# Attention, ELU and SiLU layers: VectorE's side work by budget, silu by ScalarE, y pieces kept back, sums by way of DRAM

## The chip, the cores and the metric

One core of a Trainium2 chip. The metric is device time in microseconds (us), the median of the runs. Engines: TensorE (PE; its weight loads PEld), VectorE (DVE), ScalarE (ACT), GpSimd (POOL), and SyncE (SP), whose queue issues almost all DMAs.

## The reference

Windowed causal attention with a linear bias (4 batches, 8 heads, 576 positions, head size 64), then two feed-forward layers on the 2304 tokens of width 512, each through a hidden width of 2048:

```python
scores = scale * np.matmul(q, k.transpose(0, 1, 3, 2))
mask = (rel >= 0) & (rel < 128)
scores = np.where(mask, scores + bias[None], -1000000000.0)
attn = softmax(scores)                       # exp, sum + 1e-9, divide
x = np.matmul(attn, v)                       # -> 2304 x 512
h = x @ w_in;  g = np.where(h > 0, h, np.exp(np.minimum(h, 0)) - 1);  x = g @ w_out     # layer 0
h = x @ w_in2; g = h * (1 / (1 + np.exp(-h)));                        y = g @ w_out2    # layer 1
```

Weights arrive as 64-bit floats. The kernel makes 32-bit ones of them on the chip, and every product of a feed-forward layer is three matmuls on upper and lower parts (h times gh, h times gl, lo times gh).

## The kernel before

**Attention.** 18 tiles of 128 tokens, in 36 units (a pair of tiles, a pair of heads). The loop over u (39 turns) does scores of u, normalising of u - 1, transposes of u - 2 (`turn`) and, each second turn, the mixing with v (`mix`). Between them, `point` puts up to four pieces a turn from the list `fill` into TensorE's queue: pieces of layer 0's first sweep, for the token blocks that are ready (five blocks, one of 256 and four of 512 tokens). A block has 16 h pieces (4 hidden tiles by 4) and 16 y pieces; one is three matmuls of 512 columns. What follows a piece on other engines (`bent`, `gated`, `upper`, `lower`: Exp, ELU, upper part, lower part) is put out a step at a time by `pop`. What is left of `fill`, and the last block, are done at the start of `layers`.

**Layers.** The tokens are three blocks of 768. The hidden width is cut into sweeps: 4, 6 and 6 tiles in layer 0 (the first one in the attention), 6, 6 and 4 in layer 1. A step k (k0 to k14) is one block in one sweep. It has `quad`s, one for two hidden tiles: a 2 x 2 block product by seven products m1, m2, m6, m5, m7, m4, m3 (Strassen's way, with Winograd's sums), six matmuls of 384 columns each. Its operands are seven sums of x (`make`: sums and upper and lower parts of halves of x, by VectorE and ScalarE). A step whose block was made before in this layer reloads the seven from DRAM (`reload`); one that follows on the same block keeps them. Block order: 0, 1, 2, 2, 1, 0 in layer 0, then 2, 1, 0, 0, 1, 2, 2, 1, 0. After the quads come the y pieces (`outputs`), six matmuls each, and VectorE adds their sums into `acc`.

**Order around them.** The program's order on each engine is the order in which Python issues it. After every piece `between` is called: `chain` issues one step of every open activation (line 776: bent, gated, upper, lower), in y pieces three entries of `xtasks` (the sums of the next block) follow, and `weight_step` moves weights on a stage: load, rescale (GpSimd and ScalarE), sign, join (VectorE), part (upper by ScalarE, lower by VectorE; for a pair of kind 0 four sums as well). Raw weights have four buffers, pairs three (`PAIRS`), parted out-weights seven (`OUTS`). Nothing there looks at how much VectorE has already been given. What `xtasks` still holds is issued in one go after the y pieces, and weights that a step lacks are issued in one go ahead of it. `begin` loads a half of x into the one buffer `xs`; the second half (`begin(1)`) comes after all splits of the first.

Lines: 146 and 148 rescale, 153 sign, 158 join, 167 and 168 split of weights, 189 to 192 a pair's sums, 246 and 247 split of x in the attention, 263 multiplication or maximum of the activation, 277 and 313 h and y pieces of the first sweep, 452 scores, 491 transposes, 499 and 501 their copies, 530 mixing, 684 load of x, 692 to 706 sums, 761 first ScalarE step of an activation, 771 and 774 its upper and lower part, 794 products, 881 y.

## Time and profile before

| | us |
|---|---|
| median of 3 runs | 975.95 (974.37 to 976.24) |
| the profiled execution | 972.32 |
| its span | 970.3 |
| TensorE busy | 879.8 |
| VectorE busy | 655.6 |
| ScalarE busy | 506.6 |
| GpSimd busy | 136.9 |

The profile gives each engine's busy time, for any stretch of the span; the granted clock of TensorE (1 is 2.4 GHz, 0.5 is 1.2 GHz; a number between is a mean); and for every idle time of an engine the instruction that ended it. A busy TensorE may still run at the lower clock. Some matmul records are missing from the trace, so counts are a little low.

### The profile page before, as it was taken

The page shows a single profiled execution, that of the slowest core. Times are in us where ns is not written, and L with a number is a line of the kernel's source. Part 1 is how long each engine was busy: PE and PEld are TensorE (multiplying, and loading weights), DVE is VectorE, ACT ScalarE, POOL GpSimd, SP SyncE. Part 2 cuts the span into 40 slices and gives each one's busy share as a digit, 9 for nine tenths or more (in the row PEclk, how much of TensorE's full clock was granted, in tenths as well). Part 3 has the DMA queues.
Part 4 walks back from the last instruction along what each step waited for, and adds up shares of the span by engine and source line. Part 5 has one row for each costly group of instructions (what it writes and reads, how often), then busy time and mean ns, then how long its engine had stood idle before and what let it go on. Part 6 is the DMA issues. An engine that isn't in the chain of part 4 may idle for free.

```text
span 970.3 us, 15097 instructions
## 1 busy us (share of the span) xinstructions
PE 879.8 (91%) x5520; PEld 782.0 (81%) x5520; DVE 655.6 (68%) x1471; ACT 506.6 (52%) x1191; POOL 136.9 (14%) x248
## 2 busy tenths in 40 slices
PE   6788999996469998999999878999999999999998
PEld 4566777775459998988999778798989798889997
DVE  6866566638788767987545987856687652775544
ACT  6677667645564636554434636555656251634322
POOL 7753323311110000110000101000021000000000
PEclk9789999999799999999999979999999999999999
DMA  9333273122653411335050263234224423116541
GB/s 313 96 97 122 87 230 99 51 77 86 264 202 114 179 33 44 109 136 200 14 214 1 87 268 116 99 148 193 79 109 173 164 98 130 45 44 226 207 153 66
DMA packets 54922, 125.49 MB, mean 129 GB/s; under 512 B 3648, under 2 KB 35648, under 8 KB 54848
## 3 DMA queue, kind: packets, MB, share of 16 engines
q1 hardware_dynamic: 54704, 124.40, 36.2%
q8 instruction: 43, 0.70, 0.3%
q14 instruction: 31, 0.25, 0.1%
q10 hardware_dynamic: 144, 0.13, 0.0%
HBM read 87.56 MB, written 36.96 MB: 128 GB/s over the span
## 4 chain that ended last, share of the span: by engine, by line
PE 65%; DVE 16%; ACT 10%; issue 4%; DMA 4%; POOL 1%; SPq 0%; DVEq 0%; ACTq 0%; POOLq 0%
PE y L881 31%; PE b L794 12%; PE c L794 6%; PE a L530 4%; PE y L313 3%; PE a L794 3%; PE h L277 2%; DMA wraw<-in_moe_w_out_dram 2%; PE pt L491 2%; PE s L452 2%; DVE wraw L153 2%; ACT p L465 1%; DVE gl L774 1%; DVE e L261 1%; DVE w1l L168 1%
## 5 line engine op out<-in xcount | busy, mean ns | idle before, releaser
L146 POOL TENSOR_SCALAR wraw<-wraw 128x512 f32<-128x512 f32 x60 | 46.2, 771 | 596.7 <-DMA wraw<-in_moe_w_in_dram 314.6
L771 ACT ACTIVATE gh<-e 128x384 fp32r<-128x384 f32 x168 | 85.9, 523 | 65.5 <-DVE e L263 35.7
L881 PE MATMUL y<-w1h,gl 128*128 128x512 f32 (+1 forms) x292 | 113.1, 387 | 0.7 <-DVE gl L774 0.7
L881 PE MATMUL y<-w1h,gh 128*128 128x512 f32 (+1 forms) x292 | 112.8, 386 | 0.0
L881 PE MATMUL y<-w1l,gh 128*128 128x512 f32 (+1 forms) x292 | 112.8, 386 | 0.0
L881 PE MATMUL y<-gl,w1h 128*128 128x384 f32 x288 | 99.3, 345 | 13.2 <-DVE gl L774 13.2
L894 DVE TENSOR_TENSOR acc<-y,acc 128x384 f32<-128x384 f32 (+2 forms) x85 | 50.9, 606 | 76.9 <-PE y L881 76.9
L774 DVE TENSOR_TENSOR gl<-e,gh 128x384 fp32r<-128x384 f32 x168 | 92.0, 557 | 12.9 <-ACT gh L771 10.3
L881 PE MATMUL y<-gh,w1h 128*128 128x384 f32 x288 | 98.8, 343 | 0.2 <-ACT gh L771 0.2
L881 PE MATMUL y<-gh,w1l 128*128 128x384 f32 x288 | 98.3, 341 | 0.0
L465 ACT ACTIVATE p<-p,neg 128x192 f32<-128x192 f32 (+1 forms) x144 | 62.9, 440 | 31.7 <-DVE neg L460 31.7
L801 ACT ACTIVATE hs<-b 128x384 f32<-128x384 f32 x42 | 20.4, 486 | 110.9 <-PE b L794 110.9
L511 POOL TENSOR_SCALAR p<-p,sm 128x192 f32<-128x192 f32 (+1 forms) x144 | 61.9, 449 | 100.5 <-DVE sm L469 90.7
L761 ACT ACTIVATE e<-hs 128x384 f32<-128x384 f32 x84 | 44.2, 526 | 55.6 <-DVE hs L804 55.6
L881 PEld LDWEIGHTS y<-gl,w1h 128*128 128x128 f32 x288 | 55.8, 194 | 15.1 <-DVE gl L774 15.0
L881 PEld LDWEIGHTS y<-w1h,gl 128*128 128x128 f32 x292 | 54.8, 188 | 12.4 <-DVE gl L774 1.1
L881 PEld LDWEIGHTS y<-w1l,gh 128*128 128x128 f32 x292 | 54.8, 188 | 9.4
L881 PEld LDWEIGHTS y<-w1h,gh 128*128 128x128 f32 x292 | 54.8, 188 | 9.4
L881 PEld LDWEIGHTS y<-gh,w1h 128*128 128x128 f32 x288 | 55.6, 193 | 1.0 <-ACT gh L771 1.0
L794 PE MATMUL b<-b,wah 128*128 128x384 f32 x168 | 43.6, 339 | 14.1 <-ACT b L702 12.8
L881 PEld LDWEIGHTS y<-gh,w1l 128*128 128x128 f32 x288 | 55.6, 193 | 0.0
L794 PE MATMUL b<-t,wbh 128*128 128x384 f32 x168 | 45.0, 349 | 10.2 <-DVE hs L804 10.2
(149 smaller groups left out, 2162.1 us busy)
## 6 DMA issues: line engine op xcount, KB each, us to landing
t<-d SPq DMA_DIRECT2D x24, 768.0 KB, 6.4
wraw<-in_moe_w_in_dram SPq DMA_DIRECT2D x32, 512.0 KB, 4.3
d<-t SPq DMA_DIRECT2D x20, 768.0 KB, 7.6
wraw<-in_moe_w_out_dram SPq DMA_DIRECT2D x28, 512.0 KB, 3.6
b<-d SPq DMA_DIRECT2D x18, 768.0 KB, 5.3
d<-b SPq DMA_DIRECT2D x15, 768.0 KB, 4.8
k<-in_k_dram SPq DMA_DIRECT2D x16, 384.0 KB, 5.1
v<-in_v_dram SPq DMA_DIRECT2D x18, 256.0 KB, 2.8
```

Source lines behind the costliest of these rows:

```text
L146: nc.gpsimd.tensor_scalar(f32(top), f32(top), 2.0 ** -112, 1.0, op0=ALU.mult, op1=ALU.mult)
L313: nc.tensor.matmul(tiles["ps"][:, 0:w], a[:, cs], b2[:, 0:w], start=(f == 0 and x == 0), stop=(f == FIRST_F - 1 and x == 2))
L465: nc.scalar.activation(dst, dst, AF.Exp, bias=m, scale=-1.0, accum_out=a)
L511: nc.gpsimd.tensor_scalar(dst, dst, by, 1.0, op0=ALU.mult, op1=ALU.mult)
L530: nc.tensor.matmul(ps[j * D:(j + 1) * D, i, q0:q1], vv[hp // 2][(g // 2) % 2][:, g % 2, i * P + j * D:i * P + (j + 1) * D], ptt[:, j, a * ...
L761: nc.scalar.activation(e, src, AF.Exp if layer == 0 else AF.Sigmoid)
L771: nc.scalar.activation(gh[:, s], tiles["e"], AF.Copy)
L774: nc.vector.tensor_tensor(gl[:, s], tiles["e"], f32(gh[:, s]), op=ALU.subtract)
L794: nc.tensor.matmul(t[name][:, 0:HALF], a[:, cs], x[:, j, c, :], start=(start and c == 0 and n == 0), stop=(c == 1 and n == 2), skip_group_ ...
L801: nc.scalar.activation(t[name], t[src][:, 0:HALF], AF.Copy)
L881: nc.tensor.matmul(t["ps"][:, 0:w], l, r, start=(f == 0 and x == 0), stop=(f == n - 1 and x == 2))
L894: nc.vector.tensor_tensor(dst, t["ps"][:, 0:w], dst, op=ALU.add)
```

## The change

- Attention: from the block before the last on, `point` leaves 16 pieces in `fill` (`RESERVE`). One pair's buffers (`pair0`) exist from the start, so one pair of kind 0 is parted in the attention, and two more raw weights are loaded; weight steps run in turns 24 to 35 in place of 26 to 33.
- `between(us)` gets the time that the piece's matmuls cover, subtracts what activations and additions have just been given (`spent`), and issues side work only while something of it is left (`spare`): first `urgent` (the next block's sums), where an empty place means one weight step, then weight steps, then `late_x`. `parts` splits a weight's last stage into up to five priced operations.
- A raw weight is loaded only when both raw buffers of its pair are free, and four calls later; missing out-weights are awaited hidden tile by hidden tile (`need`), not all ahead of the first y piece.
- Layer 1's activation: ScalarE computes Silu twice, into `e` and rounded into `gh`; VectorE's multiplication goes and the chain has two steps.
- The sums of step k6 (`FAR`, block 2, the first of layer 1) are made by `make_far` in k4 and k5: in place in `acc`, each operand through the one buffer `xs`, stored to DRAM, and reloaded in k5's last quad. What isn't done by then is issued in one go ahead of that quad.

```diff
-    POPS = 3
+    RESERVE = 16
-    WSLOTS = [*range(15), *range(26, 34)]
+    WSLOTS = [*range(15), *range(24, 36)]
...
+        return [(0.85, first), (0.85, second), (0.4, third), (0.7, made_of[1][2]), (0.7, done)]
...
-    room = [FIRST_F, FIRST_F]
+    room = [FIRST_F + 2, FIRST_F]
...
+    def weight_load():
+        while stage[0] < min((stage[-1] - (len(subs) > 0)) // 2 * 2 + NRAW, len(tasks)):
+            if calls[0] < at[-1].get(stage[0] - NRAW, 0) + 4:
                 break
             load_w(*tasks[stage[0]])
             at[0][stage[0]] = calls[0]
             stage[0] += 1
 
+    def weight_op():
+
+        if subs:
+            return subs.pop(0)
+        n = len(stages)
+        if stage[n] < stage[n - 1] and fits(stage[n]):
+            t = tasks[stage[n]]
+            made[t[0]] += 1
+            at[n][stage[n]] = calls[0]
+            stage[n] += 1
+            subs.extend(parts(*t))
+            return subs.pop(0)
+        for i, lag, cost in ((3, 0, 0.7), (2, 2, 0.7), (1, LAG, 0.0)):
+            if stage[i] < stage[i - 1] and calls[0] >= at[i - 1][stage[i]] + lag:
+                at[i][stage[i]] = calls[0]
+                fn, t = stages[i - 1], tasks[stage[i]]
+                stage[i] += 1
+                return cost, lambda: fn(*t)
+        return None
...
-                while n > 0 and fill:
+                while n > 0 and len(fill) > held_back[0]:
...
-                last = 2 * FIRST_F + (u >= 20) * NRAW
+                last = 2 * FIRST_F + (u >= 20) * (NRAW + 2)
...
+                            held_back[0] = RESERVE * (bi == NB - 2)
...
-            wait = [None] * (POPS * LAG if layer == 0 else 0)
-            out = spread(0) + [lambda: begin(1)] + wait + spread(1)
+            wait = [None] * (LAG if layer == 0 else 0)
+            out = spread(0) + [(0.0, lambda: begin(1))] + wait + spread(1)
...
+            def place(i, src):
+                tile_of = {}
+
+                def uppers():
+                    tile_of[0] = x = t_p.tile([P, 2, 2, HALF], F32R, tag="xs", name="xo")
+                    for c in range(2):
+                        nc.scalar.activation(x[:, 0, c, :], src[c], AF.Copy)
+                out.append((0.0, uppers))
+                out.append(None)
+                for c in range(2):
+                    out.append((0.6, lambda c=c: lower_half(tile_of[0], c, src[c])))
+                out.append((0.0, lambda: keep(layer, b, i, tile_of[0])))
+                out.extend([None] * (LAG - 2))
...
             def bent():
                 tiles["e"] = e = e_p.tile([P, HALF], F32, tag="e", name="e")
-                if below:
+                if layer == 1:
+                    nc.scalar.activation(e, src, AF.Silu)
+                    nc.scalar.activation(gh[:, s], src, AF.Silu)
+                elif below:
...
-            chains.append([bent, gated, upper, lower])
+            chains.append([bent, gated, upper, lower] if layer == 0 else [bent, lower])
...
+        def need(ok):
+            while not ok():
+                calls[0] += 1
+                weight_load()
+                op = weight_op()
+                if op:
+                    op[1]()
...
+        def between(us):
             chain()
...
             calls[0] += 1
+            weight_load()
+            spare[0] = min(spare[0] + us - spent[0], 1.0)
+            spent[0] = 0.0
+            if late_x and late_x[0] is None:
+                late_x.pop(0)
+            while spare[0] > 0:
+                op = None
+                if urgent:
+                    op = urgent.pop(0)
+                    if op is None:
+                        op = weight_op()
+                        if op is None:
+                            break
+                if op is None:
+                    op = weight_op()
+                if op is None and late_x and late_x[0]:
+                    op = late_x.pop(0)
+                if op is None:
+                    break
+                spare[0] -= op[0] + 0.03
+                op[1]()
...
-        xtasks.extend([None] * (2 * POPS) + xs0)
+        urgent.extend([None] * 3 + ops)
...
-            between("y")
+            between(0.68)
...
+                if q == nq - 1 and k + 1 == FAR:
+                    flush(late_x)
...
-                        between("h")
+                        between(1.04 if b != ORDER[layer][sw - 1 if layer == 0 else sw][0] else 1.25)
...
-                between("y")
+                between(1.04 if layer == 0 else 1.36)
+            flush(urgent)
+            if k == FAR - 3:
+                late_x.extend([None] * LAG + make_far(FAR))
```

## Rows read from the trace of the kernel before

**Rows 1.** Busy us (and instructions) of each engine by stretch; granted clock; DMA.
```profile
239.00:252.00 13.00, 0.23 (x2) 0.22 (x1) 8.60 (x16) 5.98 (x12) 1.51 (x2) 0.69 0.42 135
252.00:315.00 63.00, 50.70 (x258) 47.70 (x259) 54.82 (x101) 35.27 (x74) 5.83 (x8) 0.93 0.56 206
315.00:362.00 47.00, 47.00 (x272) 47.00 (x271) 33.87 (x69) 24.80 (x53) 0.00 (x0) 1.00 0.31 112
362.00:413.00 51.00, 47.28 (x268) 46.00 (x267) 41.27 (x80) 29.61 (x59) 5.15 (x7) 1.00 0.22 73
413.00:467.00 54.00, 50.14 (x274) 48.44 (x273) 38.11 (x69) 24.11 (x49) 3.93 (x5) 0.97 0.42 151
467.00:514.00 47.00, 47.00 (x272) 47.00 (x271) 23.94 (x47) 18.65 (x39) 0.00 (x0) 1.00 0.31 118
514.00:583.00 69.00, 57.08 (x289) 54.31 (x287) 54.14 (x105) 34.64 (x72) 4.96 (x6) 0.88 0.35 130
583.00:636.00 53.00, 47.79 (x239) 42.78 (x240) 40.59 (x76) 32.50 (x66) 4.68 (x6) 1.00 0.36 133
636.00:683.00 47.00, 47.00 (x239) 42.71 (x238) 27.47 (x55) 25.55 (x54) 0.00 (x0) 1.00 0.36 148
683.00:731.00 48.00, 46.16 (x232) 41.29 (x231) 38.01 (x70) 29.45 (x59) 5.78 (x7) 1.00 0.22 77
```

**Rows 2.** TensorE's waits: us in total, times, longest.
```profile
PE y L881 <- DVE gl L774: 13.9, 6, 5.0
PE y L313 <- ACT gh L290: 4.4, 1, 4.4
```

**Rows 3.** Order of time, 190 to 210 us: start, length, instruction, idle before.
```profile
196.25 0.72 PE L491 MATMUL pt<-ident,p 64*128 64x64 f32 x16 [1.88 <-ACT ptt L501]
205.34 1.96 PE L530 MATMUL a<-ptt,v 128*64 128x256 f32 x24
...
199.40 0.59 ACT L501 ACTIVATE ptt<-pt 128x512 f32<-128x512 f32 x1
...
200.54 1.30 DVE L247 TENSOR_TENSOR xl<-x,xh 128x512 fp32r<-128x512 f32 x2 [1.81 <-ACT xh L246]
```

**Rows 4.** VectorE's groups: count, busy us, mean ns; idle before, releaser.
```profile
L774 DVE TENSOR_TENSOR gl<-e,gh 128x384 fp32r<-128x384 f32 x168 | 92.0, 557 | 12.9 <-ACT gh L771 10.3
L153 DVE SCALAR_TENSOR_TENSOR wraw<-wraw 128x512 uint32<-128x512 uint32 x60 | 47.1, 785 | 9.0 <-POOL wraw L146 7.4 <-ACT wraw L148 1.1
...
L263 DVE TENSOR_TENSOR e<-hs,e 128x384 f32<-128x384 f32 x48 | 26.8, 558 | 12.1 <-ACT e L761 10.0
```

**Rows 5.** Busy time by stretch, as in rows 1: dense h pieces, attention's start and end.
```profile
210.00:221.00 11.00, 11.00 (x50) 9.10 (x49) 4.55 (x9) 4.46 (x10) 1.98 (x2) 1.00 0.42 139
20.00:40.00 20.00, 13.45 (x134) 9.23 (x131) 16.66 (x43) 12.06 (x38) 16.08 (x23) 0.74 0.37 120
...
187.00:208.00 21.00, 19.12 (x165) 14.46 (x164) 9.22 (x24) 10.10 (x26) 4.30 (x10) 1.00 0.05 14
```

**Rows 6.** Order of time, 236 to 252 us: the second half of x.
```profile
238.03 0.56 SPq L684 DMA_DIRECT2D xs<-xd  x1
...
245.42 0.56 DVE L692 TENSOR_TENSOR t<-xs 128x384 f32<-128x384 f32 x1 [2.83 <-DMA xs<-xd]
...
251.78 0.69 PE L794 MATMUL b<-b,wah 128*128 128x384 f32 x1 [12.77 <-ACT b L702]
```

**Rows 7.** ScalarE's groups, in the same columns; the table loads are all there are.
```profile
L761 ACT ACTIVATE e<-hs 128x384 f32<-128x384 f32 x84 | 44.2, 526 | 55.6 <-DVE hs L804 55.6
...
L389 ACT ACT_TABLE_LOAD x1 | 1.3, 1283 | 1.2 <-PEq L998 1.2
...
L761 ACT ACT_TABLE_LOAD x1 | 1.3, 1283 | 0.0
```

**Rows 8.** DMA issues: count, KB each, median us to landing.
```profile
wraw<-in_moe_w_in_dram SPq DMA_DIRECT2D x32, 512.0 KB, 4.3
...
d<-t SPq DMA_DIRECT2D x20, 768.0 KB, 7.6
```

More of the change, by code (lines that the diff above doesn't have):

```diff
@@ L172, in part, with halves, lower, parts @@
-    def part(kind, layer, f):
+    def halves(pool, tag, src, w):
+        h = pool.tile([P, w], F32R, tag=f"{tag}h", name=f"{tag}h")
+        lo = pool.tile([P, w], F32R, tag=f"{tag}l", name=f"{tag}l")
+        def lower(eng=nc.vector):
+            eng.tensor_tensor(lo, f32(src), f32(h), op=ALU.subtract)
+        return (h, lo), lambda: nc.scalar.activation(h, f32(src), AF.Copy), lower
+    def parts(kind, layer, f):
+        full = NKC * P
+        w = full // 2
         if kind == 1 or (layer == 0 and f < FIRST_F):
@@ new lines, in parts, with done @@
+            pair, upper, lower = halves(w_p if early_one else out_p[0], f"w{kind}", top, full)
+            def done():
+                lower(nc.gpsimd if early_one else nc.vector)
+                weights[kind, layer, f] = pair
+            return [(0.0, upper), (0.7, done)]
+        if f % 2 == 0:
+            pool = pair_of[layer, f + 1] = pairs.next()
+            pair, upper, lower = halves(pool, "wa", raws[kind, layer, f][:, :, 1], full)
+            def done():
+                lower()
+                weights[kind, layer, f] = pair
+            return [(0.0, upper), (0.7, done)]
@@ new lines, in first, with second, third, done @@
+        def first():
+            made_of[0][1]()
+            nc.vector.tensor_tensor(s1, a21, a22, op=ALU.add)
+            nc.vector.tensor_tensor(s2, s1, a11, op=ALU.subtract)
+        def second():
+            made_of[1][1]()
+            nc.vector.tensor_tensor(s3, a11, a21, op=ALU.subtract)
+            nc.vector.tensor_tensor(s4, a12, s2, op=ALU.subtract)
+        def third():
+            made_of[2][1]()
+            made_of[0][2]()
+        def done():
+            made_of[2][2]()
+            weights[kind, layer, f] = tuple(m[0] for m in made_of)
@@ L199, in attention_elu_silu_kernel, with part @@
+        return [(0.85, first), (0.85, second), (0.4, third), (0.7, made_of[1][2]), (0.7, done)]
+    def part(kind, layer, f):
+        for _, fn in parts(kind, layer, f):
+            fn()
+    out_p, pair_of = [], {}
+    pairs = Ring(left("pair0", 1), 1)
     tasks = []
@@ L760, in bent @@
                 else:
-                    nc.scalar.activation(e, src, AF.Exp if layer == 0 else AF.Sigmoid)
+                    nc.scalar.activation(e, src, AF.Exp)
             def gated():
                 e = tiles["e"]
+                spent[0] += 0.57 if below else 0.95
                 if below:
@@ L926, in layers @@
                 r()
-            between("y")
-            for r in after:
-                r()
-        made = [output(NB - 1, c) for c in range(NKC)]
+                between(0.68)
+            chains.append(after)
+        made_y = [output(NB - 1, c) for c in range(NKC)]
         for c, f in together(range(NKC), range(FIRST_F), 3):
-            pieces, after = made[c]
+            pieces, after = made_y[c]
             pieces.pop(0)()
@@ L936, in layers @@
                     r()
[L937 to L940 removed]
+            between(0.68)
+        flush(urgent)
         early.close()
@@ L947, in layers @@
         for k, (layer, sw, b) in enumerate(steps):
-            nq = (SWEEPS[layer][sw][1] - SWEEPS[layer][sw][0]) // 2
+            f0, f1 = SWEEPS[layer][sw]
+            nq = (f1 - f0) // 2
             left_over = None
-            if k + 1 < len(steps) and source(k + 1) == "make":
+            after = source(k + 1) if k + 1 < len(steps) else None
+            if after == "make":
                 begin, ahead = make(k + 1)
@@ L962, in layers @@
                         fn()
-                        between("h")
+                        between(1.04 if b != ORDER[layer][sw - 1 if layer == 0 else sw][0] else 1.25)
                 left_over = m4, m3
-            while [k2 for k2 in (f for f in range(*SWEEPS[layer][sw])) if (1, layer, k2) not in weights]:
-                calls[0] += 1
-                weight_step(0, (4, 3, 2, 1), 0, apart=(0, 0, 0))
-            if k + 1 < len(steps) and source(k + 1) == "make":
-                xtasks.extend(ahead)
-            elif k + 1 < len(steps) and source(k + 1) == "same":
+            if after == "make":
+                urgent.extend(ahead)
+            elif after == "same":
                 for i in range(7):
```

149 lines of the change are left out of this document (75 added, 74 removed).

## The prediction

> **What bounds the kernel now.** I read the busy times by stretch first, cut at the borders of the fifteen block products k0 to k14 [rows 1], then TensorE's waits [rows 2], then the order of time where the losses lie. TensorE is the bound: in k1, k4 and k7 (315 to 362, 467 to 514, 636 to 683 us) it is busy without a break, while VectorE is at 34, 24 and 27 of 47 us [rows 1]. So a block product costs about 47 us in either layer when nothing fails (the last sweep's, k12 to k14, are shorter and I leave them as they are). All else is loss. By that floor the stretches lose: 239 to 252 all its 13; k0 63 - 47 = 16; k2 51 - 47 = 4; k3 54 - 47 = 7; k5 69 - 47 = 22; k6 53 - 47 = 6; k8 48 - 47 = 1, and k9 and k11 look like k8 (2 more) [rows 1]. Together 58 us in k0 to k11, and 13 ahead of them. The reader is to see that losses stand where VectorE's share is highest: 54.8 of 63 in k0, 54.1 of 69 in k5, 40.6 of 53 in k6; and that its mean over the kernel would hide that. In those places the granted clock is below 1 too (0.93, 0.97 and 0.88 in k0, k3 and k5 [rows 1]), so part of the loss is TensorE at its lower level of 1.2 GHz after an idle stretch. The waits name who is late: 13.9 us for gl, the last VectorE step of an activation, and 4.4 us for gh of the last attention block [rows 2].
>
> **The attention's end.** Sixteen y pieces (three 512-column matmuls each) of the last block but one move from the attention's last four iterations to behind it. Now they cover waits there: the transposes at 196.25 waited 1.88 us, even so, for ScalarE's copy of the ones before. The last transposes stand behind a run of y pieces; without it they can start when ScalarE's copy ends, 199.40 + 0.59 = 200.0. Their two copies then stand behind the split of x on VectorE, until 200.54 + 1.30 = 201.84, and take 0.65 (half of that split) and 0.6, so the last mixing product starts at 203.1 in place of 205.34 [rows 3]: 2.2 us gained for 11 us of work moved. One weight pair is now cut in the attention, 2816 columns of VectorE, and two more raw weights are joined there. By the 557 ns of a 384-column subtraction [rows 4] the cutting takes 4.1 us, part of it in one lump ahead of a unit's scores. VectorE is at 9.2 of 21 us there [rows 5], so I charge 1.5 us (0 to 4). The mixing ends at 205.34 + 1.96 - 2.2 + 1.5 = 206.6. Behind it lie 16 kept y pieces, 16 h and 16 y pieces of the last block, 48 pieces or 144 matmuls; 50 of them took 11.0 us [rows 5], so 144 take 31.7; with the ends of groups I take 33. The wait for gh stays (the last block's four activations share one buffer): 3.5 of 4.4 us [rows 2], bounds 1 to 6, as VectorE now has more queued. The idle end of the attention may cost clock: 187 to 208 had 1.00 with its covers, 20 to 40, with idle stretches, 0.74 [rows 5]; I take 2 us (0 to 4). k0 then begins at 206.6 + 33 + 3.5 + 2 = 245, in place of 252: **7 us gained**.
>
> The Trainium skill (TensorE: Matmul & The Clock Gate, section "HAM oscillation") says that idle gaps between bursts of matmuls send the clock back to half. It speaks against emptying the attention's tail. The 0.74 of 20 to 40 us agrees, the 1.00 of 187 to 208 doesn't yet apply; by the rule the 2 us would be nearer to 4.
>
> What makes those 7 us possible is the first sum of x. Its second half is asked for only at 238.03, when the first half's last split has freed the one buffer, its first sum starts at 245.42, and TensorE, out of work, waits 12.77 us [rows 6]. After the change the splits of the first half cost about 7 us of budget at 0.68 a piece, some 10 pieces, behind 3 places for weight steps; the load has 7 more places, the second half 10 pieces: 30 of 48 pieces. The load itself took 245.42 - 238.03 = 7.4 us against 7 x 0.69 = 4.8; ScalarE and VectorE may wait 2.6 us for it, and 18 pieces of slack hide that. If they were gone, 13 us would come back.
>
> **The budget in k0 to k5.** VectorE's side work (weights, sums of x) is now issued only as far as a piece's matmuls cover it, and what activations use is subtracted. This adds no instruction and removes none; it moves backlog. In k0 VectorE worked 54.8 us [rows 1]; four raw weights that are joined in k0 now come to be joined ahead of it, 4 x 2 x 0.785 = 6.3 (the sign step [rows 4], and as much again for the join), so 48.5 remain against 47: no less than 1.5 us of loss. The 1.25 a piece for a sweep's first block issues more than TensorE covers (1.04), so I take 4 (2 to 16). k2: 41.3 of VectorE in 51: 1 (0 to 4). k3, again with 1.25 a piece and with six weights to be finished for its y: 3 (0 to 7). A raw load is no longer issued into a buffer that is still in use, so SP no longer holds up the loads and stores behind it; that I cost at nothing, since TensorE's waits name no weight load.
>
> **The block's sums by way of DRAM.** k6's operands are now made during k4 and k5, which takes some 22 VectorE steps at 0.557 [rows 4], 12 us, out of the end of k5 and into k4 (23.9 of 47 us used [rows 1]). k5's 54.1 become about 47, its floor. What is new is seven stores of 768 KB from one buffer: ScalarE's next copy into it waits until the store has landed. Stores of that size took 7.6 us from issue when queued in sevens [rows 8]; the change leaves five empty places, about 5 us. The operands sit last in the priority and get one empty place per piece; counting 59 pieces (45 of k4, 14 of k5) for at least 49 empty places (7 ahead, then 6 for each of seven), I expect four or five of seven done in time and the rest forced ahead of k5's last quad, each 7.6 + 2 x 0.557 + 2 x 0.526 [rows 4, 7, 8], some 9.8 us with ScalarE standing in front of the activations. One such stay is hidden by the banks, one not: k5 loses 6 of its 22 (0 to 28).
>
> **Silu on ScalarE.** For each half of layer 1 the sigmoid (526 ns [rows 7], as large as the Exp that share the row) and the copy to gh become two Silu of the same size; the VectorE product between them goes: 96 times 0.558 [rows 4] = 53.6 us of VectorE off layer 1, 6.7 us in each of k6 to k11. TensorE gains only in the losses there: k6 6 to 2.5, k8, k9 and k11 3 to 1. ScalarE is not the bound (32.5 of 53 in k6 [rows 1]). One table load stands ahead of the first sigmoid, 1283 ns, and none between sigmoids and copies [rows 7]; Silu needs one as well.
>
> **The sum.** Residues 4 + 1 + 3 + 6 + 2.5 + 1 = 17.5 of 58, so 40.5 gained; with the 7, 47.5. 970.3 - 47.5 = 922.8 of span; the profiled execution took 2.0 us more than its span (972.32), and the median of the runs 3.6 more than that (975.95): **928.4 us**. Bounds added the right way: all small, 9 us at the start and 56 of the 58 gained, 911; k0 as now (12 more), k3 as now (4 more) and k5 with two stores more (some 14 more), 958.
>
> **The rivals.** (a) All gaps close: the budget hits TensorE's pace and the forced stores find free room. Then 970.3 - 9 - 56 = 905 and **911**. For it: k1, k4, k7 run without a gap [rows 1]. Against it: k0's and k5's VectorE sums lie at TensorE's.
> (b) VectorE stays the bound where it is one: k0 12, k3 7, k5 14, the rest 4, so 58 becomes 37, and the start gives 7: 970.3 - 28 and the 5.6 = **948**, or 955 where the start gives nothing. For it: 48.5 against 47 in k0.
> (c) Slower: weights come late. A sweep's last weights wait for free raw buffers, are loaded in pairs, four places after their buffers came free, and take a load (4.3 us [rows 8]) and five steps over 512 columns on three engines (rescale, sign, join, copy, split), each about the sign step's 0.785 [rows 4]: some 8 us. If TensorE stands for that at the hand-overs of weights, two in each of four sweeps, it loses 64 us, the residues of k2, k3, k5 and k6 (12.5) among it: 928.4 + 64 - 12.5 = **980**. It decides from 7 or 8 hand-overs on, where 8 us each eat the 47.5 and those residues. Against it: the same hand-overs can cost no more than the 4 of k2 and the 7 of k3 now [rows 1].
> (d) Slower: Silu and Copy don't share a table. Then two switches of 1.283 us at each of 96 halves, 246 us: **1174**; it decides from 37 switches. Against it: neither Exp, Relu and Copy nor Sigmoid and Copy cost a switch [rows 7].
>
> The Trainium skill (ScalarE: Activation LUTs, section "Table sets: the hidden batching unit") says that cheap functions such as relu and copy are in every set, and that each switch costs about 2.7 us. The trace agrees with the first by its two loads, and shows 1.28 for the load alone; an estimate by the page's figure makes (d) 192 x 2.7 = 518 us, in place of 246.
>
> **How the numbers follow.** Forecast 0.62, (a) 0.10, (b) 0.19, (c) 0.07, (d) 0.02. The time is the forecast's. The range runs from between it and (a), 908, to the end of (b), 958, and leaves out (c), (d), some of (a) and the worst of the forced stores. A measurement tells 0.2% (2 us) from no change: faster 0.90 (the forecast, (a) and all but 0.01 of (b)), same 0.01, slower 0.09 ((c) and (d)).
>
> **What would show it.** No 12.8 us wait ahead of the first quad, and k0 at 243 to 248 us; TensorE idle about 8 us between 190 and 207; stretches of 50 us for k0 and k3, 53 for k5, 49 for k6. Wrong would be: stores of the far operands standing in a row at k5's last quad with more than 10 us of TensorE idle; waits for weights at the first y pieces of a sweep; more than two table loads.

## The result and the profile after

| | before | after |
|---|---|---|
| median, us | 975.16 (970.27 to 976.24) | 963.33 (960.91 to 966.37) |
| ratio after / before, 95% interval | | 0.989 [0.9845, 0.9935] |
| profiled execution; its span | 972.32; 970.3 | 966.37; 964.6 |
| TensorE busy, of the profiled span | 879.8 | 888.9 |
| VectorE busy | 655.6 | 608.0 |

The change is faster by about 1.1%, 12 us, where 47 were forecast, and 963 lies outside the range of 908 to 958. TensorE's idle time fell by 14.8 us (90.5 to 75.7), but the same 5520 matmuls kept it busy for 9.1 us longer. By the borders of the steps, in us (the forecast is 47 a step and the sum's residue):

| | begin of k0 | k0 | k2 | k3 | k5 | k6 | k8 + k9 + k11 |
|---|---|---|---|---|---|---|---|
| before | 251.8 | 62.8 | 51.7 | 53.7 | 65.7 | 52.2 | 146.6 |
| forecast | 245 | 51 | 48 | 50 | 53 | 49.5 | 142 |
| after | 256.8 | 56.8 | 48.4 | 56.3 | 54.8 | 56.2 | 149.4 |

k1, k4, k7 and k10 stayed without a gap (47.0, 47.0, 46.4 and 46.4 us), so TensorE's floor was read rightly. k2 and k5 came near their forecast. k0 began later, and k3, k6 and k9 (49.5 before) got longer. Below are the windows of after that answer to [rows 1, 5], cut at its own step borders (columns as in rows 1; the first three are the end of the attention and the last block's y pieces).

```profile
208.00:212.40 4.40, 4.39 (x37) 3.14 (x33) 1.89 (x3) 1.18 (x3) 0.00 (x0) 0.61 0.00 0
234.00:245.00 11.00, 4.59 (x13) 2.08 (x11) 10.69 (x18) 5.91 (x12) 4.48 (x4) 0.74 0.52 209
245.00:257.00 12.00, 12.00 (x44) 9.44 (x45) 6.69 (x12) 3.55 (x6) 0.65 (x1) 0.81 1.00 379
...
256.80:313.60 56.80, 48.79 (x260) 46.05 (x259) 44.01 (x82) 32.61 (x68) 4.72 (x7) 0.97 0.27 91
409.00:465.30 56.30, 51.04 (x272) 48.12 (x271) 41.60 (x76) 28.27 (x56) 6.45 (x8) 0.97 0.49 173
512.30:567.10 54.80, 49.09 (x272) 48.45 (x271) 40.38 (x84) 28.57 (x59) 2.63 (x4) 0.94 0.51 197
567.10:623.30 56.20, 49.46 (x235) 43.09 (x234) 39.53 (x70) 33.34 (x68) 5.26 (x7) 0.97 0.37 136
718.50:769.90 51.40, 48.63 (x236) 43.16 (x235) 28.72 (x47) 22.46 (x47) 4.88 (x6) 0.97 0.47 164
```

The longer busy time stands ahead of k0. From 160 us to k0's begin, before and then after, TensorE's idle time fell by 5.0 us (20.2 to 15.2), while as many matmuls took 10.0 us more, at a granted clock of 0.88 for 0.94:

```profile
160.00:251.80 91.80, 71.63 (x556) 54.42 (x554) 58.87 (x150) 50.48 (x126) 20.72 (x40) 0.94 0.26 81
```

```profile
160.00:256.80 96.80, 81.60 (x557) 60.40 (x556) 64.16 (x168) 52.83 (x134) 20.38 (x39) 0.88 0.43 152
```

In the steps, the reader is to see VectorE's column. In k0 it fell from 54.8 of 63 to 44.0 of 57; in k6 it is at 39.5 of 56, in k9 at 28.7 of 51. VectorE has room in these steps, and TensorE waits for it all the same (TensorE's waits, first of before, beside [rows 2], then of after):

```profile
PE b L794 <- DVE hs L804: 10.2, 11, 1.9
PE b L794 <- ACT hs L801: 5.9, 5, 1.5
```

```profile
PE pt L540 <- ACT ptt L550: 19.2, 14, 3.4
PE b L901 <- DVE hs L912: 11.6, 13, 2.9
PE b L901 <- ACT hs L908: 9.5, 8, 5.4
PE y L998 <- ACT w1h L167: 5.1, 3, 2.7
PE y L362 <- ACT gh L339: 4.9, 3, 2.3
```

The 12.8 us for the first sums of x are gone, and so are the 13.9 us for gl at the y pieces (0.8 us left). The waits for hs, the addition that reads a product's bank, are as large as before, with a longest of 2.9 for 1.9 us. ScalarE's copy hs (5.4 us of it in one place, k5) and w1h are longer. The two table loads of [rows 7] are two still, the second now ahead of the first Silu, so rival (d) is out:

```profile
L860 ACT ACT_TABLE_LOAD x1 | 1.3, 1283 | 0.0
```

The first places to look at are the head of k6 and the last quad of k5, each in order of time by engine (start, length, instruction, idle before and its releaser):

```profile
579.63 0.62 PE L901 MATMUL b<-t,wbh 128*128 128x384 f32 x2 [2.93 <-DVE hs L912]
...
576.54 0.55 DVE L1012 TENSOR_TENSOR acc<-y,acc 128x384 f32<-128x384 f32 x1
577.01 0.68 DVE L158 SCALAR_TENSOR_TENSOR wraw<-wraw 128x512 uint32<-128x512 uint32 x1
578.42 0.69 DVE L166 TENSOR_TENSOR w1l<-wraw,w1h 128x512 fp32r<-128x512 f32 x1 [0.72 <-ACT w1h L167]
579.03 0.55 DVE L912 TENSOR_TENSOR hs<-b,hs 128x384 f32<-128x384 f32 x1
...
577.73 0.66 ACT L167 ACTIVATE w1h<-wraw 128x512 fp32r<-128x512 f32 x1 [2.04 <-DVE wraw L158]
```

```profile
536.16 1.01 PE L901 MATMUL b<-t,wch 128*128 128x384 f32 x2 [5.43 <-ACT hs L908]
...
534.80 0.94 ACT L801 ACTIVATE xo<-acc 128x384 fp32r<-128x384 f32 x2 [3.94 <-DMA d<-xo]
535.64 0.47 ACT L908 ACTIVATE hs<-b 128x384 f32<-128x384 f32 x1
```

At 577 one weight goes back and forth: VectorE joins it, ScalarE, which had waited 2.04 us for that, copies it, VectorE waits 0.72 us for the copy, subtracts, and only then adds hs, for which TensorE stands 2.93 us. The prediction's sum has no term for this: it adds up VectorE's busy time, and here VectorE holds TensorE up by what is ahead in its queue, partly while it stands idle itself.

### The profile page after: what moved, and what is told of

It reads as the page before. It is cut to its first block, busy times and chain, and to the rows that moved or that the text cites. A ratio compares the mean times of both kernels' runs of the same rounds, so it can differ in the third digit from the quotient of the medians.

```text
span 964.6 us, 15023 instructions
## 1 busy us (share of the span) xinstructions
PE 888.9 (92%) x5520; PEld 786.2 (82%) x5520; DVE 608.0 (63%) x1375; ACT 500.1 (52%) x1191; POOL 134.3 (14%) x248
## 5 line engine op out<-in xcount | busy, mean ns | idle before, releaser
L881 DVE TENSOR_TENSOR gl<-e,gh 128x384 fp32r<-128x384 f32 x168 | 94.2, 565 | 81.0 <-ACT gh L861 76.0
L146 POOL TENSOR_SCALAR wraw<-wraw 128x512 f32<-128x512 f32 x60 | 44.1, 736 | 574.4 <-DMA wraw<-in_moe_w_in_dram 277.2
L1012 DVE TENSOR_TENSOR acc<-y,acc 128x384 f32<-128x384 f32 (+2 forms) x85 | 51.4, 607 | 72.4 <-PE y L998 72.4
L908 ACT ACTIVATE hs<-b 128x384 f32<-128x384 f32 x42 | 20.2, 481 | 85.3 <-PE b L901 85.3
L998 PEld LDWEIGHTS y<-gl,w1h 128*128 128x128 f32 x288 | 54.8, 190 | 1.2 <-DVE gl L881 1.2
L540 PEld LDWEIGHTS pt<-ident,p 64*128 64x128 f32 x544 | 23.8, 152 | 37.2 <-POOL p L560 27.3
L901 PE MATMUL b<-t,wch 128*128 128x384 f32 x168 | 45.3, 351 | 9.5 <-ACT hs L908 9.5
L877 ACT ACTIVATE gh<-e 128x384 fp32r<-128x384 f32 x72 | 36.8, 524 | 32.7 <-DVE e L312 18.7
```

The source lines that it names most:

```text
L146: nc.gpsimd.tensor_scalar(f32(top), f32(top), 2.0 ** -112, 1.0, op0=ALU.mult, op1=ALU.mult)
L540: nc.tensor.transpose(ps[:, x, j, i, :], pt[half, j, e, c - x * PAD:c - x * PAD + P], ident[half, half])
L877: nc.scalar.activation(gh[:, s], tiles["e"], AF.Copy)
L881: nc.vector.tensor_tensor(gl[:, s], tiles["e"], f32(gh[:, s]), op=ALU.subtract)
L901: nc.tensor.matmul(t[name][:, 0:HALF], a[:, cs], x[:, j, c, :], start=(start and c == 0 and n == 0), stop=(c == 1 and n == 2), skip_group_ ...
L908: nc.scalar.activation(t[name], t[src][:, 0:HALF], AF.Copy)
```

## The experiments

Two theories stand against each other. By the prediction's, a step loses what VectorE's amount of work exceeds TensorE's. By the other, it loses by the order in the queues: an instruction that waits stands ahead of one that TensorE needs. The times are medians, with the ratio to the kernel before on the same chip; small differences are read from ratios and from kernels of the same chip, as the kernel before itself moved between 971.7 and 975.2 from chip to chip. Step lengths come from one profile of each kernel. In five kernels that are the same up to k3 (after, e4, e5, e9, e11), k0 begins at 254.6 to 256.8 and takes 54.5 to 56.8, k3 takes 55.8 to 56.3, and the waits at the last block's y pieces are 4.6 to 6.4 us; after itself is at the upper end of each, so differences as small as these are not read as an edit's. The edits up to e12 are to after, but for e7's, which is to the kernel before.

**e1: the attention's pair in parts.** The parting of a pair is issued in its parts between the turns' other work, not at once.

```diff
+                t = tasks[stage[i]]
+                if i == len(stages) and t[0] == 0 and t[2] >= FIRST_F:
+                    asubs.extend(parts(*t))
+                else:
+                    stages[i - 1](*t)
...
+                if asubs:
+                    asubs.pop(0)[1]()
```

> The changed kernel, but the pair that is parted in the attention is put out one operation at a time, two in a turn behind the unit's scores, not all in one go ahead of them. In the changed kernel the scores of units 30 and 31 come 1.9 and 4.7 us later than their place (3.0 and 5.9 us against the kernel before, 1.1 up to unit 29), with the 3.5 us lump of VectorE ahead of unit 30. Theory A (what stands ahead in VectorE's order costs, not how much work there is): the lump's 4.7 us go, clock loss included; the last mixing ends at 207.5 to 208.5 in place of 212.4, k0 starts at 252, the whole is 959 us against 963. Theory B (the added work itself is too much for these turns): the delay is spread over units 30 to 35 but stays, last mixing at 211 to 213, the whole 963.

958.77 us, ratio 0.986 [0.9833, 0.9887]. The attention's last mixing ends at 206.7 in place of 212.4 (the prediction had 206.6), and k0 begins at 250.7 in place of 256.8. What e1 takes away is this lump, ahead of a unit's scores (after):

```profile
160.03 0.41 DVE L200 TENSOR_TENSOR wraw<-wraw 128x256 f32<-128x256 f32 x1
...
162.43 0.68 DVE L166 TENSOR_TENSOR wdl<-wraw,wdh 128x512 fp32r<-128x512 f32 x1
163.03 0.35 DVE L509 CUSTOM_DVE_ANT_0 p<-s,biasa 128x192 f32<-128x192 f32 x1
...
163.77 1.52 PE L501 MATMUL s<-k,q 64*64 64x192 f32 x10 [1.81 <-issue]
```

Seven VectorE steps, 3.1 us, and with them the scores' reading is late, TensorE stands 1.81 us, and each later unit is late too. So 3 us of VectorE in one piece cost 5.7 us at the mixing's end (in the whole 0.3% by the ratios, or 4.7 us against e3 on the same chip). In after the last mixing product takes 4.04 us, at a granted clock of 0.61 over 208 to 212.4, against 1.96 before [rows 3]. That is not the lump's: in e1 it takes as long (its clock is 0.57 there).

```profile
202.62 4.07 PE L584 MATMUL a<-ptt,v 128*64 128x256 f32 x24
```

**e2: no pieces kept back.** `RESERVE = 0`.

> The changed kernel with no pieces kept back (RESERVE 0): the last four turns of the attention have their y pieces again, and 32 pieces are left for the sums of the first block. The prediction's reason (the kept pieces hide the first sums): the last mixing ends at about 215, and the sums, 30 pieces long, just don't fit, so TensorE waits 5 to 12 us ahead of k0, which starts at 262 or later; the whole is 968 to 975. Theory C (the emptied tail loses at the lower clock what the kept pieces cover): the tail has a clock of 1, the 48 pieces take as long wherever they stand, k0 starts within 2 us of 256.8, the whole is 962 to 965.

962.08 us, ratio 0.9889 [0.9861, 0.9917], as after. k0 begins 9.7 us earlier (247.1) and takes 64.0 us in place of 56.8: TensorE now waits in k0 for weights (its waits there: us, times, longest; in after 2.7, once).

```profile
PE y L998 <- ACT w1h L167: 9.0, 4, 4.0
```

The kept pieces gain next to nothing. The 12.8 us wait for the sums doesn't come back without them; weights that haven't had their time come late instead. And keeping them back costs clock at the attention's end. With these pieces between its last turns, as here, it is at 1.00 over 187 to 214.6, and the last mixing product takes what it took before the change:

```profile
212.69 1.96 PE L579 MATMUL a<-ptt,v 128*64 128x256 f32 x24
```

**e3: true empty places.** The places behind the load of x give VectorE nothing, in place of a weight step.

```diff
-            wait = [None] * (LAG if layer == 0 else 0)
+            wait = ["hold"] * (0 if layer else 11 if k == 0 else 7)
...
+            held = urgent[:1] == ["hold"]
+            if held:
+                urgent.pop(0)
...
-                if urgent:
+                if urgent and not held and urgent[0] != "hold":
```

> The changed kernel, with the empty places between the load of a half of x and its first sum made true ones: each lasts a whole piece (11 for the first block, 7 for the others), where one empty place now is used up by each weight operation, several to a piece. Theory A (the sum that waits for its load stands ahead of the last attention block's activations in VectorE's order; it began its wait at 230.1 and ran at 232.4, and the activation's step that had its input at 229.4 came at 234.0): the five waits ahead of and in the last block's y pieces (6.4 us) become 2 to 3, k0 starts at 252 to 254, the whole is 959. Theory D (the four activations go through one buffer, 4 us each, and that sets the y pieces): the waits stay at 5 to 6.5 us, the whole 963.

963.48 us, ratio 0.99 [0.9873, 0.9927]. k0 begins at 257.0, and TensorE still waits 5.9 us at the last block's y pieces (6.4 in after). VectorE's wait for that load (2.29 us in after) is gone here and TensorE's waits are not, so it doesn't set them. What is left is theory D, the chain of that block's activations through one buffer, which this run doesn't test by itself.

**e4: no detour by way of DRAM.** `FAR = -10`.

> The changed kernel without the detour by DRAM: the sums of k6 are made like those of k7 and k8, at k5's end. If the detour gains what the prediction says, k5 and k6 (54.8 and 56.2 us in the changed kernel, 65.7 and 52.2 in the one before) become 60 to 64 and 54 to 56 and the whole 6 to 10 us longer (970). If its forced stores (5.4 us of TensorE idle at k5's last quad, and the lower clock after it) cost as much as it takes away from k5's end, k5 stays at 53 to 57 and the whole is within 2 us of 963.

977.22 us, ratio 1.0049 [1.0024, 1.0073]. k5 falls to 48.4 us and k6 rises to 76.0, 124.4 together against 111.0 in after. So in this kernel the detour is worth 13 us, seen in k6 and not in k5. It is mostly late weights that it saves: in e4's k6 TensorE waits 11.0 us for w1h (0.4 in after), and its clock is 0.73 over 590 to 633.6. Against the kernel before it looks different: there 9.8 us of waits for gl stood at k5's end, and k5 and k6 took 117.9 together. The budget without the detour makes them 124.4, with it 111.0; the budget alone, on the kernel before, wasn't run.

**e5: layer 1's product back on VectorE.** Sigmoid, product and copy as before.

```diff
-                    nc.scalar.activation(e, src, AF.Silu)
-                    nc.scalar.activation(gh[:, s], src, AF.Silu)
+                    nc.scalar.activation(e, src, AF.Sigmoid)
...
-            chains.append([bent, gated, upper, lower] if layer == 0 else [bent, lower])
+            chains.append([bent, gated, upper, lower])
```

> After, with layer 1's activations as before the change: Sigmoid on ScalarE, the product on VectorE (96 more of about 0.56 us, counted in the budget), the copy on ScalarE. The prediction put the two Silu at 3.5 us in k6 and 2 in k8, k9 and k11 together, so this would be 5.5 us longer than after: about 969. Rival: k6 loses its time by the order of the work in the queues (a weight's subtraction standing ahead of an activation's step) and not by VectorE's amount; then 53 us of VectorE work more in layer 1 move it by under 2 us: 962 to 965, k6 still 56.

959.26 us, ratio 0.9853 [0.9835, 0.9872]: with 53 us of VectorE work more it is not slower than after, which neither theory allowed. The ratios' intervals overlap; the steps tell more. k6 is longer (58.8 for 56.2), k8, k9 and k11 shorter (142.7 together, where seven kernels with the two Silu as in after have 149.0 to 149.5).

**e7: Silu alone, on the kernel before.**

```diff
-                    nc.scalar.activation(e, src, AF.Exp if layer == 0 else AF.Sigmoid)
+                    if layer == 1:
+                        nc.scalar.activation(e, src, AF.Silu)
+                        nc.scalar.activation(gh[:, s], src, AF.Silu)
+                    else:
+                        nc.scalar.activation(e, src, AF.Exp)
...
-            chains.append([bent, gated, upper, lower])
+            chains.append([bent, gated, upper, lower] if layer == 0 else [bent, lower])
```

> The kernel before with one part of the change alone: layer 1's sigmoid, product and copy become two Silu. The prediction put it at 5.5 us, k6 from 53 to 49.5 and k8, k9 and k11 by 2 together: about 969.5 against 975. k5 (69 us) stays, since it is of layer 0. If VectorE's amount is not what limits k6 to k11, no change: 973 to 976.

979.05 us, ratio 1.0048 [1.0031, 1.0064]: alone, this part costs time, above all in k6 (57.7 for 52.2). VectorE's waits point to why, and e9 tests it. First after, then e5, then e7; us, times, longest:

```profile
DVE gl L881 <- ACT gh L861: 76.0, 82, 2.6
```

```profile
DVE gl L882 <- ACT gh L878: 8.2, 12, 1.6
```

```profile
DVE gl L778 <- ACT gh L763: 68.9, 71, 2.6
```

One step of every open chain is issued after each piece. With four steps a copy stood one piece ahead of its subtraction; with two, both Silu and VectorE's subtraction are issued one piece apart, and ScalarE hasn't finished the second. VectorE stands there, 76 us in all, with the next hs behind it. That is more than the 53.6 us of work that Silu took from it.

**e9: one empty place behind the two Silu.**

```diff
-            chains.append([bent, gated, upper, lower] if layer == 0 else [bent, lower])
+            chains.append([bent, gated, upper, lower] if layer == 0 else [bent, lambda: None, lower])
```

> After, with an empty place between the two Silu and VectorE's last step of an activation in layer 1. In after VectorE waits 76.0 us (82 times) at that step for ScalarE's second Silu, 8.2 us where the product is back on VectorE, and a long step's next addition (hs, for which TensorE waits) stands behind it. If that wait is why Silu costs time, it falls below 20 us, k8, k9 and k11 fall from 48.8, 51.4 and 49.2 to about 47.3 and k6 from 56.2 to 54, some 8 us in all: 955. If it is ScalarE that is late (two Silu in a row, 1.05 us, ahead of its copies of b), nothing changes: 962 to 965.

955.35 us, ratio 0.982 [0.9799, 0.9842]. VectorE's wait falls to this, and k6 to 51.3 us; k8, k9 and k11 are 144.8 together:

```profile
DVE gl L881 <- ACT gh L861: 18.5, 27, 1.0
```

So most of that loss was the wait; k8, k9 and k11 stayed above the 142 expected. With it mended, Silu is worth 3.9 us against e5 by the times, 3.2 by the ratios, whose intervals still overlap. That is near the forecast 5.5 by luck: k6 gains 7.5 (forecast 3.5), and k8, k9 and k11 lose 2.1 (forecast a gain of 2).

**e8: copy and subtraction of a weight one piece apart.** `PAUSE` is an empty operation that ends what is issued after a piece; it stands so for w1 and for wa.

```diff
-            return [(0.0, upper), (0.7, done)]
+            return [(0.0, upper), PAUSE, (0.7, done)]
...
-                if op is None:
+                if op is None or op is PAUSE:
```

> After, with a weight's copy on ScalarE and its subtraction on VectorE issued one piece apart. In after they are issued back to back, so that VectorE stands at the subtraction until ScalarE has copied, with an activation's step behind it: at k6's start TensorE stands 2.9 us so. If that order is the loss, k6 falls by some 3 us, k3 by 2 and k0 by 1: 957 to 959. If the amount of work or late weights set it, it is as after (962 to 965), or up to 3 us longer, as the weights get done a piece later.

951.67 us, ratio 0.9764 [0.9739, 0.9789], the most that one edit gave, and twice what was expected. k0 falls from 56.8 (54.5 at the least) to 51.4, about the forecast; k9 from 51.4 to 47.7. k6 falls from 56.2 to 53.9, but k7 rises from 46.4 to 48.4, so there nothing is gained in sum. VectorE's waits for a weight's copy, in after and then in e8:

```profile
DVE w1l L166 <- ACT w1h L167: 22.2, 23, 2.7
...
DVE wal L166 <- ACT wah L167: 14.6, 13, 4.0
```

```profile
DVE w1l L166 <- ACT w1h L167: 8.1, 7, 2.8
DVE wal L166 <- ACT wah L167: 7.5, 5, 4.0
```

The work is the same; 21 us of standing at these two subtractions went. The empty place also ends what is issued after that piece, so less is put out at once; but e6 below, which puts out less and leaves the two together, gains nothing. k3 (55.7) hardly moved.

**e6: an allowance of 1.04 for a sweep's first block too.**

> After, with an allowance of 1.04 us for each h piece in the first block of a sweep too, in place of 1.25. The long steps of after are just those first blocks: k0 56.8, k3 56.3, k6 56.2, k9 51.4 us, with waits for VectorE's activation steps. If the allowance is what issues too much, these four fall by some 2 to 4 us each, about 10 us in all: 953. Rival: the weights need that allowance; then they come later, and waits for w1h at the first y pieces (2.0 to 2.8 us each in after) grow by more than what is gained: 965 to 975.

965.24 us, ratio 0.9907 [0.989, 0.9924]. k0 (54.1) is hardly below the 54.5 that it takes without the edit, k3 is 56.9 and k6 58.8, and waits for w1h grow from 5.1 to 9.6 us. The larger allowance is not the fault: work that it doesn't issue comes late.

**e10: the last block's first two lower halves on VectorE.** In `lower`, `eng = nc.vector` in place of GpSimd for those two.

> After, with the last attention block's first two lower halves made by VectorE in place of GpSimd (1.3 us each there). That block's four activations share one buffer, so their chains follow one another at about 4 us each against 2.8 us of h pieces. If that chain sets the y pieces of the block (6.4 us of TensorE's waits between 234 and 245 us in after), each chain is 0.6 us shorter and 1 to 2 us of them go: k0 starts 1 to 2 us earlier. If VectorE's queue sets them, they stay or grow by up to 1 us, as VectorE gets two steps more. Against after's 963 that is 961 to 962, or 963 to 964.

962.03 us, ratio 0.9888 [0.9866, 0.9911]. TensorE's waits at those y pieces fall from 6.4 to 4.4 us and k0 begins at 253.7. But e11, which is as after up to there, has 4.6 and 254.6, and the total is after's. That the chain through the one buffer sets these pieces is likely, and not shown.

**e11: fewer empty places behind the stores.** The edit leaves three places in place of five behind each store (the expectation's text begins with a wrong count).

```diff
-                out.extend([None] * (LAG - 2))
+                out.extend([None] * (LAG - 4))
```

> After, with four places fewer held empty behind each store of the far operands through the single buffer (one in place of... three in place of five for each of seven). In after TensorE stands 5.4 us at k5's last quad, where the stores that are left are forced and ScalarE waits for a store to land; a store lands 3.6 us after its issue. If the places decide, all seven are done by then and k5 falls by 4 to 5.4 us: 958 to 959. If VectorE's budget has no room for them, as many are left and k5 stays at 54.8.

957.91 us, ratio 0.9847 [0.982, 0.9874]. k5 is 48.0 for 54.8: no store is forced any more. k6 gives 1.8 us back.

**e12: e1, e8, e9, e10 and e11 together.**

> After with the four edits together (the attention's pair cut in parts between units, copy and subtraction of a weight one piece apart, the empty place behind Silu, fewer empty places behind the stores, lower halves by VectorE). If the causes are apart they add up: 6 + 8 (k0, k6) + 8 + 5 + 1 less what the second and third share (some 3) gives about 25 us below after: 938 to 942. If late weights take their place, waits for w1h and for the weights of a quad grow and it ends near 948.

933.48 us, ratio 0.9588 [0.956, 0.9616], 4.5 us below the expected range. In ratios, the five singly give 0.3, 1.3, 0.7, 0.0 and 0.4%, 2.7 together, and e12 has 3.0. That is about a sum, but each single difference leans on after's own ratio, which is known to 0.45% only. The steps agree: k0 is 51.4 as in e8, k5 48.4 (48.0 in e11), k6 49.3, and k8, k9 and k11 are 140.8. k0's begin does not add up: it is 251.9, and e1 alone had 250.7. Left are the begin of k0 (251.9) and k3 (55.7). Three more kernels went to these two, as edits to e12.

**e13: the last block's y pieces by hidden block first.**

```diff
-        for c, f in together(range(NKC), range(FIRST_F), 3):
+        for c, f in [(c, f) for f in range(FIRST_F) for c in range(3)] + [(3, f) for f in range(FIRST_F)]:
```

> The kernel with the edits together, and the last attention block's first twelve y pieces by hidden block first and then by output (three pieces of one hidden block, 2.1 us, in a row) in place of three hidden blocks of one output in a row. There TensorE waits 5.2 us in four places between 230 and 240 us, and the next 20 matmuls follow one another by 0.43 us in place of 0.23, 4 us more. If the chain of the activations sets the time and the clock falls only by the bursts between waits, the same chains are covered better: k0 starts at 247 to 249 in place of 251.9 and the total is 929 to 931. If the clock stays at its lower level, as the waits are only moved, k0 starts at 251 to 252: 933.

931.57 us, ratio 0.9572 [0.9549, 0.9596]. k0 begins at 247.8 in place of 251.9 (and at 248.1 in e15 for 250.4 in e14). The waits are still 4.9 us in all, in seven places where there were four; TensorE is busy 6.6 of 10 us from 230 to 240 in place of 4.8. The clock is the difference. Windows of e12, then e13:

```profile
240.00:247.00 7.00, 7.00 (x20) 5.54 (x21) 6.86 (x14) 3.74 (x6) 0.00 (x0) 0.62 1.01 368
```

```profile
230.00:240.00 10.00, 6.57 (x25) 4.14 (x24) 9.74 (x19) 5.18 (x11) 0.20 (x1) 1.00 0.85 347
240.00:250.00 10.00, 8.56 (x39) 6.61 (x37) 6.63 (x13) 5.52 (x10) 0.67 (x2) 1.00 1.01 366
```

e12 ran 240 to 247 without a gap at a mean of 0.62, most of it at 1.2 GHz: up to 245.2 us its matmuls follow one another by 0.43 us, 11 of them and not the 20 of the expectation, and then by 0.23. From 160 us to k0's begin TensorE is busy 79.1 us in e12 and 75.4 in e13, with as many matmuls: 3.7 us. Of the 4.1 us k0 gives 2.8 back (54.2 for 51.4; in e15 2.1, for e14's 51.3). A reason would be that its sums and weights have less time ahead of it, as in e2. The total's interval overlaps with e12's, so the gain is shown at k0's begin and not in the whole.

**e14: lower halves of layer 0's w1 by GpSimd in the layers.**

```diff
-                lower(nc.gpsimd if early_one else nc.vector)
+                lower(nc.gpsimd if early_one or layer == 0 else nc.vector)
...
-            return [(0.0, upper), PAUSE, (0.7, done)]
+            return [(0.0, upper), PAUSE, (0.7 * layer, done)]
```

> The kernel with the edits together, and the lower halves of layer 0's w1 weights in k0 to k5 made by GpSimd (about 1.3 us each) in place of VectorE (0.69). k3 is still 55.7 us there and k0 51.4, with waits for late w1h of 1.85 and 2.76 us, and VectorE busy 26.1 of k3's first 30 us. If VectorE's amount makes them late, k3 falls to some 53 and k0 to some 49: 928 to 930. If the order of the steps or the loads make them late, no change (931 to 935), or waits for w1l take the place of those for w1h.

930.97 us, ratio 0.9568 [0.954, 0.9595]. The interval overlaps with e12's. k3 falls to 53.3 from e12's 55.7, or from 54.3 in e13, whose k3 is issued as e12's: 1.0 to 2.4 us. TensorE's wait for w1h there (1.8 us in e12) is gone, and 0.8 for GpSimd's w1l has come. Whether VectorE's amount made it late isn't shown, as the edit also takes the price of these steps out of the budget and VectorE no longer stands for their copies. The amount itself fell little: VectorE is busy 603.4 us for 606.5, and not 12 times 0.69 less. Beside GpSimd's subtraction VectorE's sign step takes 1.80 us, and 0.69 where GpSimd stands:

```profile
417.34 1.51 POOL L166 TENSOR_TENSOR w1l<-wraw,w1h 128x512 fp32r<-128x512 f32 x1 [8.30 <-ACT w1h L167]
...
412.07 0.69 DVE L153 SCALAR_TENSOR_TENSOR wraw<-wraw 128x512 uint32<-128x512 uint32 x1
...
417.59 1.80 DVE L153 SCALAR_TENSOR_TENSOR wraw<-wraw 128x512 uint32<-128x512 uint32 x1
```

In k0 (51.3) nothing is gained: of e12's wait of 2.8 us for w1h, 1.3 is left, and 1.3 for GpSimd's w1l has come (TensorE's waits in k0 of e14):

```profile
PE y L1009 <- POOL w1l L166: 1.3, 1, 1.3
PE y L1009 <- ACT w1h L167: 1.3, 1, 1.3
```

**e15: both.**

> Both of these edits on the kernel with the edits together. If both causes hold, 924 to 928; if neither, as that kernel: 931 to 935.

929.18 us, ratio 0.9543 [0.9522, 0.9564]: the best, 4.6% below the kernel before; that the two add up isn't shown, as its interval overlaps with each one's, and narrowly with e12's.

## Why the prediction was wrong

The span after was 964.6 where the sum had 922.8. By the table, k0's begin missed by 12 us, k0 and k3 by 6 each, k6 by 7, and k8, k9 and k11 by 7 together; k2 and k5 by 2 in all. So three steps of the prediction failed: the price of the attention's end, "it moves backlog", and the gain by Silu.

- **The floor and the sum's form: right.** Gaps and the lower clock behind them are all the loss, and steps without either are at 47.0 or 46.4 us. The borders in [rows 1] were rough: k5 took 65.7 and not 69, k8, k9 and k11 146.6 and not 144; about the same in sum. e15 reaches 929, about where the sum ended, but by seven edits more; that isn't the forecast come true.
- **The attention's end (7 us gained; 5 lost): a failed step.** Its waits were seen, its prices were not. The lump of parting: 1.5 us charged, bounds 0 to 4; e1 shows 5.7. The prediction saw the lump ("part of it in one lump ahead of a unit's scores") but priced it as VectorE's share. The wait for gh: 3.5 charged, 6.4 measured for that block's gh and gl. The clock: 2 us charged, bounds 0 to 4; TensorE is 10.0 us longer busy with the same matmuls in after, of which e1 takes 4.2 away with the lump. What is left is in two places: the emptied attention (the last mixing product takes 2.1 us more, and 1.96 again in e2) and the last block's y pieces (3.7 us by e13 against e12). That the mixing ended at 206.7 in e1, as the sum had it, is luck: e1 has a loss of clock where the sum had 1.5 us for the lump. The rule on the clock that speaks against emptying the tail, in the Trainium skill (TensorE: Matmul & The Clock Gate, section "HAM oscillation"), was weighed at 2 us of 4; the 0.61 at 208 to 212 and 0.74 at 234 to 245 us agree with its direction.
- **The sums no longer late: right, for little.** The 12.8 us wait went. But e2 shows that it goes without the kept pieces too, and that what they buy is time for the weights.
- **"It moves backlog" (k0 4, k3 3 us left): a failed step.** k0 lost 9.8 (7.5 at the least in kernels that are the same up to there) and k3 9.3 us. The amount was forecast well (48.5 of VectorE in k0; it was 44.0) and did not decide: in k0 order did, as e8 brings it to 51.4. `parts` issues a weight's copy and subtraction one right behind the other. The code before did so too, and VectorE stood 14.9 and 10.5 us for w1h and wah; after has 22.2 and 14.6, of which 3.6 of w1l lie in 567 to 600 us, k6's head, and 3.5 in k9, with hs behind them; and in k0's first 5 us it stands 4.5 us for GpSimd's rescale of a weight. That price has no term in the sum, though the trace of before could have given one. For k3 order gives nothing that shows (e12 has 55.7 still); e14 takes 1.0 to 2.4 us of it, and what makes its weights late stays open.
- **The detour (k5 loses 6 of 22): right in size, by its own working.** k5 lost 7.8, of which 5.4 are one forced stay of ScalarE for a store, as forecast ("one not" hidden), and the last two of seven operands came there. A store landed in 3.6 us at the median, not 7.6 (the first took 9.5). What was missed is that without it the budget would bring k6's weights late: 13 us by e4.
- **Silu (5.5 us gained): wrong sign, a failed step.** e7 shows 4.8 us of loss. The 53.6 us of VectorE were counted as gone, but the shorter chain put 76 us of standing in their place. With an empty place (e9) the total is 3.2 to 3.9 us better than with the product on VectorE (e5), but not in the steps where the sum had it.
- **The rivals.** (b) was nearest with 948, but for another reason than it gave. (c), late weights, was seen in its mechanism, 5.1 us in three places and not 64. The bounds for the steps were set by busy times; a wait in a queue, which can cost more than the work it replaces, was in none, and so the range ended too low. Nor did a measurement tell 0.2%: the interval of after's ratio is 0.9% wide.

## What to carry to other kernels

Where engines run in order, read a change of the side work's schedule instruction by instruction: for each one that waits for another engine, find what stands behind it and who needs that, and put at least one slot between a producer on one engine and its consumer on another. A busy share well below the step's length doesn't say that the engine is harmless. When work is taken out of a chain, look at which places of the chain go with it, since those may have been the time in which the other engine caught up. And compare an engine's busy time too, not only its waits: here 14.8 us less idle time gave 5.7 us, since the same matmuls ran longer.

## What the runs showed of the hardware

- Idle stretches of 0.6 to 2.3 us between single matmuls at the last block's y pieces brought the granted clock to 0.74 over 234 to 245 us of after, and the dense matmuls behind them ran on at the lower level for 4.7 us more (e12, 240.5 to 245.2 us; a mean of 0.62 over 240 to 247). About the idle time of e12 (4.9 us against 5.2), cut by bursts of three pieces into gaps of 1.1 us at most, left it at 1.00 (e13).
- Pieces of other work between waits kept the clock: with 16 of them in the attention's last turns it is at 1.00 (e2, 187 to 214.6 us), and without them at 0.92 over 187 to 208 and 0.61 over 208 to 212.4 (after).
- Silu and Copy alternated on ScalarE without a table load between them: one load of 1283 ns ahead of the first Silu, and 525 ns for a Silu over 384 columns, as for a sigmoid [rows 7].
- VectorE was slower beside GpSimd's work: in e14 VectorE's sign step took 1.80 and 1.81 us beside GpSimd's subtractions and 0.69 alone. Twelve subtractions of 0.69 us moved to GpSimd took 3.1 us off VectorE's busy time, and 1.46 us each there. VectorE's step that reads h from a product's bank in the attention took 0.69 us with GpSimd busy beside it and without (after, eight times each).
